# Masks of two attention units as four matmuls on 32-row tiles, and keys' one-hot clusters turned two tiles at a time

## The chip, the cores and the metric

The kernel runs on one core of one Trainium2 chip. The metric is the device time of one execution in microseconds (us), as the median of repeated runs. Engines are named as in the profile: PE is TensorE (matmuls), PEld its weight loads, DVE VectorE, ACT ScalarE, POOL GpSimd, SP SyncE; SPq and POOLq are the queues that issue DMAs.

## The reference

An attention whose mask comes from clusters, and then a mixture of experts. Cut to what matters here:

```python
# q, k, v: (4, 8, 768, 64), centroids: (8, 16, 64)
q_assign = np.argmax(np.einsum('bhsd,hcd->bhsc', q_n, c_n), axis=-1)
k_assign = np.argmax(np.einsum('bhsd,hcd->bhsc', k_n, c_n), axis=-1)
mask = q_assign[:, :, :, None] == k_assign[:, :, None, :]
scores = np.where(mask, scale * (q @ k.T), -1000000000.0)
attn = softmax(scores); x = attn @ v
# then: each of the 3072 tokens goes to one of 8 experts (argmax of a cosine),
out = gate * (relu(x @ w1[e]) @ w2[e])      # w1: (8, 512, 1024), w2: (8, 1024, 512)
```

A query sees the keys that fall into its own cluster, of 16.

## The kernel before, in words

**Stages.** Attention first (to about 445 us), then the routing tables (to about 478 us), then 28 blocks of 128 tokens through the experts (to the end). The change touches the attention alone.

**Rounds, units and groups.** Heads are worked two at a time: a round is one batch and one pair of heads, 16 rounds in all (`pairs`). The 768 tokens are six tiles of 128 (NJ = 6, tile j). A unit (`units`) is one round, one half of the queries (hq, 384 columns) and one tile j of 128 keys, for both heads; there are 192. Six units with the same half of the queries are a group (GU), whose output gathers in one bank `o_ps`.

**The mask as a matmul.** For each token, head, and queries or keys, `oh` holds a one-hot row of its cluster, and in column C a constant (−1 for queries, +1 for keys). Turned by TensorE, they become `qH` and `kH`, with each head's clusters on partitions of their own; `qH` is multiplied by 2^60 on the way (L283). The product kH·qH is then 0 where clusters agree and −2^60 where they don't, and the scores are added to it in the same bank. In `oh` each tile and head has 64 columns (D), of which 17 are used, so a tile of 128 tokens turns into 128 partitions, head 0 on 0 to 63 and head 1 on 64 to 127; `turn_hot` (L272) makes six transposes for the queries and six for the keys.

**A unit.** `scores(i)` (L330 to 345) issues two bf16 mask matmuls (one per head, 64 contraction rows each, 384 columns) and two f32 score matmuls (kT, qT) on the same 64-row tiles, into the two banks of one `s_ps` buffer; there are two such buffers (`psS`, bufs=2), so a unit's mask waits for the exponential of the unit two before. `expo(i)` (L347) takes the exponential on ScalarE. `attend(i)` (L352) multiplies by the values on TensorE and adds up the probabilities on VectorE (`acc`, L367 and L377). At a group's end `total` (L381) sums `acc` over partitions on TensorE, ScalarE copies it (L393), and `divide` (L396) takes the reciprocal (L401) and writes `xT` (L402) on VectorE. `rows` (L413) turns it back.

**The preparation of the next round** is cut into ten pieces (`prep_pieces`, list at L309): turns of q and k with copies by ScalarE (L227) and VectorE (L229), `products` with the centroids (L235), `assign` (turn L248, maximum L256, equality L257, and on GpSimd a preference that breaks ties, L258), `choose` (maximum L264, one-hot L265), nothing, `turn_hot` of queries (copy on VectorE L283), `turn_hot` of keys (copy on ScalarE L285), and `mean` (L298, L306), which is added to the output so that an empty row becomes the mean of the values.

**The order is written out by hand** (`manual_schedule`, L515, for TensorE, VectorE and ScalarE). The loop at L524 takes two units per iteration, six iterations per round: scores and exponentials of the two units ahead, a piece of the preparation, every third iteration `rows` of the last group, `attend` of the two units at hand, every third iteration `total` and `divide`, a second piece, and in some rounds a piece of the routing (`route_pieces`, L430 to 505). So of a round's iterations the first two hold the turns and products, the third `assign` and `choose`, the fourth the queries' `turn_hot` at its end, the fifth the keys' `turn_hot` and `mean`. Small outputs of TensorE share two banks (`misc`, bufs=2), used in turn.

Engines take their instructions in order, so whatever stands behind a waiting one waits too.

Of the kernel before, what the change touches and what calls it, by code (L numbers as in the profile page):

```python
# [9 lines left out]
F32 = mybir.dt.float32  # L10
BF16 = mybir.dt.bfloat16
# [24 lines left out]
def kernel(  # L36
# [67 lines left out]
    with ExitStack() as at:  # L104
# [61 lines left out]
        nc.vector.tensor_scalar(tok_t, tok_i, 6, None, ALU.arith_shift_right)  # L166
        nc.vector.tensor_scalar(tok_hi, tok_t, 1, None, ALU.add)

        ohs = [const.tile([P, NJ // 2, 4, 2, D], BF16, name=f"oh{i}") for i in range(2)]
        for oh in ohs:  # L170
            nc.gpsimd.memset(oh, 0.0)
            for t in range(2):
                nc.gpsimd.memset(oh[:, :, 2 * t : 2 * t + 2, :, C : C + 1], (-1.0, 1.0)[t])

        def unit_rows(dst, src, n):

# [32 lines left out]
        def prep_pieces(n):  # L209

            hp = pairs[n][1]
            t = ld[n]
            oh = ohs[n % 2]

            def turn(nm, half):
                if half == 0:
                    t[nm + "T"] = trp.tile([P, S], F32, tag=nm + "T", name=nm + "T")
                bk = misc()
                for j in range(NJ // 2):
                    nc.tensor.transpose(  # L220
                        bk[:, P * j : P * j + P],
                        t[nm][:, NJ // 2 * half + j].rearrange("p h d -> p (h d)"),
                        ident,
                    )
                dst = t[nm + "T"][:, HS * half : HS * half + HS]
                if nm == "q":
                    nc.scalar.activation(dst, bk[:, 0:HS], ACTF.Copy, scale=scale)  # L227
                else:
                    nc.vector.tensor_copy(dst, bk[:, 0:HS])  # L229

            def products():

                bk = misc()
                for i in range(4):
                    nc.tensor.matmul(  # L235
                        bk[2 * C * i : 2 * C * i + 2 * C, 0:HS],
                        lhsT=cnB[:, hp],
                        rhs=t["qk"[i // 2] + "T"][:, HS * (i % 2) : HS * (i % 2) + HS],
                        start=True,
                        stop=True,  # L240
                    )
                t["asT"] = smp.tile([P, HS], F32, tag="asT", name="asT")
                nc.scalar.copy(t["asT"], bk[:, 0:HS])

            def assign():
                bk = misc()
                for u in range(NJ // 2):
                    nc.tensor.transpose(  # L248
                        bk[:, P * u : P * u + P], t["asT"][:, P * u : P * u + P], ident
                    )  # L250
                shp = [P, 4 * NJ, C]
                asn = bk[:, 0 : 4 * NJ * C].rearrange("p (g c) -> p g c", c=C)
                amax = smp.tile(shp[0:2], F32, tag="amax", name="amax")
                sel = smp.tile(shp, BF16, tag="sel", name="sel")
                t["sel"] = sel
                nc.vector.tensor_reduce(amax, asn, axis=AXX, op=ALU.max)  # L256
                nc.vector.tensor_tensor(sel, asn, bc(amax, shp, 2), ALU.is_equal)  # L257
                nc.gpsimd.tensor_tensor(sel, sel, bc(prefc, shp, 1), ALU.mult)  # L258

            def choose():  # L260

                shp = [P, 4 * NJ, C]
                pm = smp.tile(shp[0:2], BF16, tag="pm", name="pm")
                nc.vector.tensor_reduce(pm, t["sel"], axis=AXX, op=ALU.max)  # L264
                nc.vector.tensor_tensor(  # L265
                    oh.rearrange("p u t h c -> p (u t h) c")[:, :, 0:C],
                    t["sel"],
                    bc(pm, shp, 2),
                    ALU.is_equal,
                )  # L270

            def turn_hot(i, nm):  # L272
                hot = t[nm + "H"] = trp.tile([P, S], BF16, tag=nm + "H", name=nm + "H")
                bk = misc().bitcast(BF16)
                for j in range(NJ):
                    half, u = divmod(j, NJ // 2)
                    nc.tensor.transpose(
                        bk[:, P * j : P * j + P],
                        oh[:, u, 2 * i + half].rearrange("p h c -> p (h c)"),
                        identb,  # L280
                    )
                if nm == "q":
                    nc.vector.tensor_scalar(hot, bk[:, 0:S], BIG, None, ALU.mult)  # L283
                else:
                    nc.scalar.copy(hot, bk[:, 0:S])  # L285

            def values():

                v = t["v"]
                vs = smp.tile([P, NJ // 2, 2, D], F32, tag="vs", name="vs")  # L290
                nc.gpsimd.tensor_tensor(vs, v[:, 0 : NJ // 2], v[:, NJ // 2 :], ALU.add)  # L291
                nc.gpsimd.tensor_tensor(vs[:, 0], vs[:, 0], vs[:, 1], ALU.add)
                nc.gpsimd.tensor_tensor(vs[:, 0], vs[:, 0], vs[:, 2], ALU.add)
                t["vs"] = vs

            def mean():
                bk = misc()
                nc.tensor.matmul(  # L298
                    bk[:, 0:1],
                    lhsT=t["vs"][:, 0].rearrange("p h d -> p (h d)"),  # L300
                    rhs=epsc,
                    start=True,
                    stop=True,
                )
                t["ev"] = smp.tile([P, 1], F32, tag="ev", name="ev")
                nc.vector.tensor_copy(t["ev"], bk[:, 0:1])  # L306


            return [  # L309
                lambda: (turn("q", 0), turn("k", 0), values()),  # L310
                lambda: turn("q", 1),
                lambda: turn("k", 1),
                products,
                assign,
                choose,
                None,
                lambda: turn_hot(0, "q"),
                lambda: turn_hot(1, "k"),
                mean,
            ]  # L320

# [7 lines left out]

        def scores(i):  # L330

            n, hq, j = units[i]
            t = ld[n]
            s_ps = un[i]["s_ps"] = psS.tile([P, 2, 512], F32, tag="s_ps", name="s_ps")
            for l, r, first in (("kH", "qH", True), ("kT", "qT", False)):
                for h in range(2):
                    rows = slice(D * h, D * h + D)
                    nc.tensor.matmul(  # L338
                        s_ps[:, h, 0:HS],
                        lhsT=t[l][rows, P * j : P * j + P],  # L340
                        rhs=t[r][rows, HS * hq : HS * hq + HS],
                        start=first,
                        stop=not first,
                    )

        def expo(i):
# [168 lines left out]
        with tc.manual_schedule(engines={EngineType.PE, EngineType.DVE, EngineType.Activation}):  # L515
            for piece in prep_pieces(0):
                if piece:
                    piece()
            for m in range(2):
                scores(m)  # L520
                expo(m)


            for i in range(0, len(units) + 6, 2):  # L524
                g, part = divmod(i, GU)
                if i < len(units) and i % (2 * NJ) == 0:
                    n = i // (2 * NJ)
                    assert not prepare
                    if n + 1 < len(pairs):
                        load(n + 1)  # L530
                        prepare = prep_pieces(n + 1)
                    if n == 1:

                        for w in range(2):
                            nc.sync.dma_start(
                                out=w1s[w], in_=moe_w1[0].rearrange("(c p) f -> p c f", p=P)
                            )
                            nc.sync.dma_start(
                                out=w2s[w], in_=moe_w2[0].rearrange("(c p) d -> p c d", p=P)
                            )  # L540
                for m in range(i + 2, min(i + 4, len(units))):
                    scores(m)
                    expo(m)
                prep()
                if part == 4 and g > 0:
                    rows(g - 1)
                for m in range(i, min(i + 2, len(units))):
                    attend(m)
                if part == 0 and g > 0:
                    total(g - 1)  # L550
                    divide(g - 1)
                prep()
                if routing:
                    routing.pop(0)()
                if part == 4 and g > 0 and g % (2 * NHP) == 0:
                    assert not routing
                    routing = route_pieces(g // (2 * NHP) - 1)
# [252 lines left out]
```

## Time and profile before

| what | value |
|---|---|
| median of five runs | 904.37 us (903.69 to 905.53) |
| the profiled execution's own time | 904.47 us |
| its span, first to last instruction | 902.70 us |
| TensorE matmul busy | 842.4 us (93%) |
| TensorE weight loads busy | 495.5 us (55%) |
| VectorE busy | 357.1 us (40%) |
| ScalarE busy | 301.7 us (33%) |
| GpSimd busy | 127.6 us (14%) |
| score matmuls L338, f32 | 768 records, 486 ns each |
| mask matmuls L338, bf16 | 384 records, 329 ns each |
| turns of one-hot rows L277 | 192 records |

How to read it: busy times are unions of records, and matmul records overlap, since a matmul is shown from its start to a modelled end; the distance from one start to the next tells for how long the array was taken. An f32 matmul is two records, each with a weight load of its own. In a row, "64*128" is the shape of the array's part that is used (rows by columns), "64x384" the moving operand. Times in the timeline count from the first instruction. The TensorE clock is full (1.00) in the attention stage from about 24 us on.

### The profile page before, as it was taken

The numbers are of one execution on the slowest core, as the hardware profiler recorded it, in microseconds if no ns is written. First come the engines' busy times: TensorE is split into PE (matmuls) and PEld (weight loads), VectorE is DVE, ScalarE is ACT, GpSimd is POOL, SyncE is SP. The second block draws the span as 40 slices with busy tenths as digits, with TensorE's granted clock in tenths as the row PEclk, the third lists the DMA queues.
The fourth block names the chain that finished last, engine by engine and source line by source line (L and its number), as shares of the span: only waits on it lengthen the run. The fifth ranks groups of instructions, "written<-read, shape, count | busy, mean of one in ns | idle before, by whom it ended". The sixth has DMA issues, their size and how long they took to land.

```text
span 902.7 us, 12774 instructions
## 1 busy us (share of the span) xinstructions
PE 842.4 (93%) x5207; PEld 495.5 (55%) x5207; DVE 357.1 (40%) x488; ACT 301.7 (33%) x485; POOL 127.6 (14%) x171
## 2 busy tenths in 40 slices
PE   4999999999999999999628999999999999999996
PEld 2444444444444444444216777767676776767672
DVE  3577777877777877687750000000000000000000
ACT  3545556654566555755330111111111111111110
POOL 4011010211111111110021011110101010101010
PEclk8999999999999999999957999999999999999998
DMA  9822211322213122020011390756565656405610
GB/s 241 308 54 53 53 36 36 108 53 53 53 36 106 36 54 53 19 88 1 1 70 36 117 321 24 261 192 256 192 256 189 260 199 258 152 24 199 233 36 21
DMA packets 105645, 106.85 MB, mean 118 GB/s; under 512 B 77157, under 2 KB 77157, under 8 KB 105072
## 3 DMA queue, kind: packets, MB, share of 16 engines
q1 hardware_dynamic: 100928, 92.30, 32.1%
q0 software_dynamic: 4480, 13.65, 4.1%
q8 instruction: 43, 0.70, 0.3%
q14 instruction: 18, 0.15, 0.0%
q10 hardware_dynamic: 176, 0.05, 0.0%
HBM read 152.11 MB, written 13.64 MB: 184 GB/s over the span
## 4 chain that ended last, share of the span: by engine, by line
PE 38%; issue 29%; DMA 19%; DVE 9%; ACT 2%; POOL 1%; SPq 0%; POOLq 0%; DVEq 0%
DMA out_dram<-y,sidx 19%; PE s_ps L338 15%; PE o_ps L358 12%; DVE den L401 4%; PE misc L220 3%; PE misc L385 2%; PE misc L235 2%; PE misc L419 1%; DVE acc L377 1%; DVE xT L402 1%; ACT den L393 1%; PE misc L441 1%; PE misc L248 1%; DVE qH L283 1%; PE misc L298 1%
## 5 line engine op out<-in xcount | busy, mean ns | idle before, releaser
L714 PEld LDWEIGHTS h_ps<-xTm,w1s 128*128 128x128 f32 x1792 | 204.7, 193 | 22.1 <-DVE xTm L704 19.7
L714 PE MATMUL h_ps<-xTm,w1s 128*128 128x128 f32 x1792 | 208.8, 278 | 3.0 <-DMA w1s<-in_moe_w_dram 3.0
L727 PE MATMUL y_ps<-w2s,hT 128*128 128x512 f32 x448 | 201.2, 592 | 0.0
L349 ACT ACTIVATE prob<-s_ps 128x768 f32<-128x768 f32 x192 | 153.2, 811 | 100.4 <-PE s_ps L338 78.1
L704 DVE COPY xTm<-x_ps 128x512 f32<-128x512 f32 x28 | 19.4, 691 | 381.0 <-PE x_ps L702 381.0
L338 PE MATMUL s_ps<-qT,kT 64*128 64x384 f32 x768 | 156.5, 486 | 0.0
L358 PE MATMUL o_ps<-prob,v 128*64 128x384 f32 x768 | 145.1, 499 | 0.0
L377 DVE TENSOR_TENSOR acc<-acc,prob 128x768 f32<-128x768 f32 x128 | 130.2, 1017 | 4.9
L727 PEld LDWEIGHTS y_ps<-w2s,hT 128*128 128x128 f32 x448 | 81.0, 190 | 81.3 <-issue 81.3
L721 ACT ACTIVATE hT<-h_ps 128x512 f32<-128x512 f32 x56 | 33.4, 597 | 243.8 <-PE h_ps L714 243.8
L401 DVE RECIPROCAL den<-den 128x384 f32<-128x384 f32 x32 | 81.7, 2552 | 30.8 <-ACT den L393 30.8
L338 PEld LDWEIGHTS s_ps<-qT,kT 64*128 64x128 f32 x768 | 69.3, 190 | 21.4 <-issue 21.4
L736 POOL DMA_INDIRECT out_dram<-y,sidx x28 | 28.4, 1014 | 356.4 <-ACT y L735 350.4
L358 PEld LDWEIGHTS o_ps<-prob,v 128*64 128x64 f32 x768 | 46.5, 136 | 56.7 <-issue 55.1
L338 PE MATMUL s_ps<-qH,kH 64*128 64x384 bf16 x384 | 64.0, 329 | 1.6 <-ACT prob L349 1.3
L735 ACT ACTIVATE y<-y_ps,xin 128x512 f32<-128x512 f32 x28 | 19.2, 687 | 136.1 <-PE y_ps L727 129.9
L291 POOL TENSOR_TENSOR vs<-v 128x384 f32<-128x384 f32 x16 | 17.2, 1073 | 221.6 <-DMA v<-in_v_dram 221.6
L338 PEld LDWEIGHTS <-kH 64*128 64x128 bf16 x384 | 19.4, 94 | 51.7 <-issue 37.0
L229 DVE COPY kT<-misc 128x384 f32<-128x384 f32 x32 | 17.7, 554 | 54.1 <-PE misc L220 54.1
L258 POOL TENSOR_TENSOR sel<-sel,prefc 128x384 bf16<-128x384 bf16 x16 | 24.2, 1514 | 102.6 <-DVE sel L257 102.6
L393 ACT COPY den<-misc 128x384 f32<-128x384 f32 x32 | 15.3, 479 | 50.3 <-PE misc L385 50.3
L674 POOL DMA_INDIRECT xin<-x_rows,gidx x28 | 28.9, 1032 | 12.3 <-issue 8.2
(146 smaller groups left out, 511.9 us busy)
## 6 DMA issues: line engine op xcount, KB each, us to landing
w1s<-in_moe_w_dram SPq DMA_DIRECT2D x30, 2048.0 KB
w2s<-in_moe_w_dram SPq DMA_DIRECT2D x30, 2048.0 KB
x_rows<-xr SPq DMA_DIRECT2D x4, 1539.0 KB
q<-in_q_dram SPq DMA_DIRECT2D x32, 192.0 KB
k<-in_k_dram SPq DMA_DIRECT2D x32, 192.0 KB
v<-in_v_dram SPq DMA_DIRECT2D x32, 192.0 KB
xin<-x_rows,gidx POOLq DMA_INDIRECT x28, 6.8
out_dram<-y,sidx POOLq DMA_INDIRECT x28, 7.0
```

Of the source, the lines that this page charges most:

```text
L220: nc.tensor.transpose(bk[:, P * j : P * j + P], t[nm][:, NJ // 2 * half + j].rearrange("p h d -> p (h d)"), ident,)
L338: nc.tensor.matmul(s_ps[:, h, 0:HS], lhsT=t[l][rows, P * j : P * j + P], rhs=t[r][rows, HS * hq : HS * hq + HS], start=first, stop=not first,)
L349: nc.scalar.activation(d["prob"], d["s_ps"][:, :, 0:HS], ACTF.Exp)
L358: nc.tensor.matmul(g["o_ps"][D * h : D * h + D, 0:HS], lhsT=ld[n]["v"][:, j, h], rhs=d["prob"][:, h], start=(j == 0), stop=(j == NJ - 1),)
L377: nc.vector.tensor_tensor(g["acc"], g["acc"], d["prob"], ALU.add)
L393: nc.scalar.copy(d["den"], bk[:, 0:HS])
L401: nc.vector.reciprocal(d["den"], d["den"])
L674: nc.gpsimd.indirect_dma_start(out=xin, out_offset=None, in_=x_rows[:], in_offset=bass.IndirectOffsetOnAxis(ap=gidx[:, j : j + 1], axis=0) ...
L714: nc.tensor.matmul(bk[:, m : m + P], lhsT=w1s[j % 2][:, c, f0 + m : f0 + m + P], rhs=d["xT"][:, P * c : P * c + P], start=(c == 0), stop=( ...
L721: nc.scalar.activation(d["hT"][:, f0 : f0 + 512], bk, ACTF.Relu)
L727: nc.tensor.matmul(bk, lhsT=d["hT"][:, P * c : P * c + P], rhs=w2s[j % 2][:, c], start=(c == 0), stop=(c == KF - 1),)
L736: nc.gpsimd.indirect_dma_start(out=out[:], out_offset=bass.IndirectOffsetOnAxis(ap=sidx[:, j : j + 1], axis=0), in_=y, in_offset=None, bou ...
```

## The change

`scores(i)` now issues two units at once. Their four masks come first, each on a 32-row tile of its own, into the four banks of the two `s_ps` buffers; then the four score matmuls as before, on 64-row tiles. For that `oh` is laid out anew with 32 columns for a tile and head. The queries' one-hot rows are written twice (r = 0, 1), so that a turned tile holds head 0, head 1, head 0, head 1 on four groups of 32 partitions: six transposes as before. The keys' rows are written once, with two tiles side by side in a transpose: three transposes instead of six, and `kH` is half as wide; an even tile j lies on partitions 0 to 63, an odd one on 64 to 127. `choose` writes the one-hot rows by three instructions (twice the queries, once the keys) instead of one. `assign` writes its three turned tiles interleaved, so that the groups lie in the order that the new `oh` wants. The calls of `scores` move: it's called once for two units, ahead of both exponentials, and no longer between them.

```diff
-        ohs = [const.tile([P, NJ // 2, 4, 2, D], BF16, name=f"oh{i}") for i in range(2)]
+        ohs = [const.tile([P, 3 * NJ, 2, 2 * C], BF16, name=f"oh{i}") for i in range(2)]
...
             def assign():
                 bk = misc()
+                tiles = bk[:, 0:HS].rearrange("p (t u w) -> p t u w", t=4, w=2 * C)
                 for u in range(NJ // 2):
-                    nc.tensor.transpose(
-                        bk[:, P * u : P * u + P], t["asT"][:, P * u : P * u + P], ident
-                    )
+                    nc.tensor.transpose(tiles[:, :, u], t["asT"][:, P * u : P * u + P], ident)
...
+                G = 2 * NJ
+                hots = oh.rearrange("p (t j) h c -> p t (j h) c", j=NJ)[:, :, :, 0:C]
+                qs = oh[:, 0:G].rearrange("p (j r) h c -> p j r h c", r=2)[:, :, :, :, 0:C]
+                for r in range(2):
+                    nc.vector.tensor_tensor(
+                        qs[:, :, r],
+                        t["sel"][:, 0:G].rearrange("p (j h) c -> p j h c", h=2),
+                        bc(pm[:, 0:G].rearrange("p (j h) -> p j h", h=2), [P, NJ, 2, C], 3),
+                        ALU.is_equal,
+                    )
                 nc.vector.tensor_tensor(
-                    oh.rearrange("p u t h c -> p (u t h) c")[:, :, 0:C],
-                    t["sel"],
-                    bc(pm, shp, 2),
-                    ALU.is_equal,
+                    hots[:, 2], t["sel"][:, G:], bc(pm[:, G:], [P, G, C], 2), ALU.is_equal
                 )
...
+            def turn_hot_k():
+                hot = t["kH"] = trp.tile([P, HS], BF16, tag="kH", name="kH")
+                bk = misc().bitcast(BF16)
+                for j in range(NJ // 2):
+                    nc.tensor.transpose(
+                        bk[:, P * j : P * j + P],
+                        oh[:, 2 * NJ + 2 * j : 2 * NJ + 2 * j + 2].rearrange("p j h c -> p (j h c)"),
+                        identb,
+                    )
+                nc.scalar.copy(hot, bk[:, 0:HS])
...
         def scores(i):
-            n, hq, j = units[i]
-            t = ld[n]
-            s_ps = un[i]["s_ps"] = psS.tile([P, 2, 512], F32, tag="s_ps", name="s_ps")
-            for l, r, first in (("kH", "qH", True), ("kT", "qT", False)):
+            for m in (i, i + 1):
+                un[m]["s_ps"] = psS.tile([P, 2, 512], F32, tag="s_ps", name="s_ps")
+            for m in (i, i + 1):
+                n, hq, j = units[m]
                 for h in range(2):
-                    rows = slice(D * h, D * h + D)
+                    r = D * (j % 2) + 2 * C * h
                     nc.tensor.matmul(
-                        s_ps[:, h, 0:HS],
-                        lhsT=t[l][rows, P * j : P * j + P],
-                        rhs=t[r][rows, HS * hq : HS * hq + HS],
-                        start=first,
-                        stop=not first,
+                        un[m]["s_ps"][:, h, 0:HS],
+                        lhsT=ld[n]["kH"][r : r + 2 * C, P * (j // 2) : P * (j // 2) + P],
+                        rhs=ld[n]["qH"][r : r + 2 * C, HS * hq : HS * hq + HS],
+                        start=True,
+                        stop=False,
+                    )
+            for m in (i, i + 1):
+                n, hq, j = units[m]
+                for h in range(2):
+                    nc.tensor.matmul(
+                        un[m]["s_ps"][:, h, 0:HS],
+                        lhsT=ld[n]["kT"][D * h : D * h + D, P * j : P * j + P],
+                        rhs=ld[n]["qT"][D * h : D * h + D, HS * hq : HS * hq + HS],
+                        start=False,
+                        stop=True,
                     )
...
+                if i + 2 < len(units):
+                    scores(i + 2)
                 for m in range(i + 2, min(i + 4, len(units))):
-                    scores(m)
                     expo(m)
```

The clears of `oh` on GpSimd follow its new shape, and the queries' turn (`turn_hot_q`) keeps its six transposes and its copy with the factor 2^60.

More of the change, by code (lines that the diff above doesn't have):

```diff
@@ L167 @@
         nc.vector.tensor_scalar(tok_hi, tok_t, 1, None, ALU.add)
-        ohs = [const.tile([P, NJ // 2, 4, 2, D], BF16, name=f"oh{i}") for i in range(2)]
+        ohs = [const.tile([P, 3 * NJ, 2, 2 * C], BF16, name=f"oh{i}") for i in range(2)]
         for oh in ohs:
             nc.gpsimd.memset(oh, 0.0)
-            for t in range(2):
-                nc.gpsimd.memset(oh[:, :, 2 * t : 2 * t + 2, :, C : C + 1], (-1.0, 1.0)[t])
+            nc.gpsimd.memset(oh[:, 0 : 2 * NJ, :, C : C + 1], -1.0)
+            nc.gpsimd.memset(oh[:, 2 * NJ :, :, C : C + 1], 1.0)
         def unit_rows(dst, src, n):
@@ L265, in choose, with turn_hot_q @@
                 nc.vector.tensor_tensor(
-                    oh.rearrange("p u t h c -> p (u t h) c")[:, :, 0:C],
-                    t["sel"],
-                    bc(pm, shp, 2),
-                    ALU.is_equal,
-                )
-            def turn_hot(i, nm):
-                hot = t[nm + "H"] = trp.tile([P, S], BF16, tag=nm + "H", name=nm + "H")
+                    hots[:, 2], t["sel"][:, G:], bc(pm[:, G:], [P, G, C], 2), ALU.is_equal
+                )
+            def turn_hot_q():
+                hot = t["qH"] = trp.tile([P, S], BF16, tag="qH", name="qH")
@@ L274, in turn_hot @@
                 bk = misc().bitcast(BF16)
                 for j in range(NJ):
-                    half, u = divmod(j, NJ // 2)
                     nc.tensor.transpose(
                         bk[:, P * j : P * j + P],
-                        oh[:, u, 2 * i + half].rearrange("p h c -> p (h c)"),
+                        oh[:, 2 * j : 2 * j + 2].rearrange("p r h c -> p (r h c)"),
                         identb,
                     )
[L282 to L285, printed above, removed]
+                nc.vector.tensor_scalar(hot, bk[:, 0:S], BIG, None, ALU.mult)
@@ L316, in prep_pieces @@
                 None,
-                lambda: turn_hot(0, "q"),
-                lambda: turn_hot(1, "k"),
+                turn_hot_q,
+                turn_hot_k,
                 mean,
@@ L518 @@
                     piece()
+            scores(0)
             for m in range(2):
-                scores(m)
                 expo(m)
@@ L540 @@
                             )
+                if i + 2 < len(units):
+                    scores(i + 2)
                 for m in range(i + 2, min(i + 4, len(units))):
-                    scores(m)
                     expo(m)
```

## The prediction

> **What bounds the kernel now.** I read the busy table first, then the stretches, then single instructions. In the attention stage (25 to 445 us) TensorE is busy 98% of each 100 us and no other engine passes 76%:
>
> ```profile
> core 0: us, PE busy (x) PEld busy (x) DVE busy (x) ACT busy (x) POOL busy (x), PEclk, DMA share, GB/s
> 100.00:200.00 100.00, 98.00 (x662) 44.90 (x660) 74.24 (x95) 56.51 (x93) 15.53 (x22) 1.00 0.25 64
> 200.00:300.00 100.00, 97.60 (x662) 45.06 (x661) 75.59 (x95) 56.82 (x93) 13.64 (x21) 1.00 0.25 64
> ```
>
> So a change to TensorE's instructions counts here, except where TensorE already waits. The expert stage after 480 us is not touched. The timeline of TensorE shows the pair of units that the change rewrites (start, length, instructions; the mask is the bf16 row):
>
> ```profile
> 204.08 0.35 PE L298 MATMUL misc<-epsc,vs 128*128 128x1 f32 x2 [0.41 <-DVE qH L283]
> 204.36 0.34 PE L338 MATMUL s_ps<-qH,kH 64*128 64x384 bf16 x2
> 204.53 0.81 PE L338 MATMUL s_ps<-qT,kT 64*128 64x384 f32 x4
> 205.18 0.33 PE L338 MATMUL s_ps<-qH,kH 64*128 64x384 bf16 x2
> 205.34 0.81 PE L338 MATMUL s_ps<-qT,kT 64*128 64x384 f32 x4
> 206.08 0.55 PE L419 MATMUL misc<-ident,xT 128*128 128x128 f32 x3
> 206.56 0.54 PE L358 MATMUL o_ps<-prob,v 128*64 128x384 f32 x2
> ```
>
> Only starts can be subtracted, since the matmuls overlap. Two masks occupy the array 0.16 us (205.18 to 205.34): the two heads run side by side on two 64-row tiles. An f32 matmul is two records of 0.32 us, again both heads side by side, so a unit's scores take 0.64. With 0.17 for the first mask, a pair of units takes 0.173 + 0.645 + 0.163 + 0.642 = 1.623 us. There are 96 such pairs.
>
> **What a change of tile shape costs.** By the single records, the last score record above starts at 205.668 and streams 0.32, but the transposes (128*128) start at 206.082: 0.094 of gap. The same gap stands wherever the shape in the rows changes: last transpose 206.357 + 0.109 to the value matmul (128*64) at 206.559 is 0.093; last value record 207.584 + 0.322 to the mask (64*128) at 208.003 is 0.097; 128*64 to 128*32 (L358 to L235) 0.094. Where the shape stays (L358 to L385, both 128*64) there is none: 211.543 to 211.866 is just the 0.32. And after a change the first weight load isn't hidden:
>
> ```profile
> 204.04 0.30 PEld L298 LDWEIGHTS misc<-epsc,vs 128*128 128x128 f32 x2 [1.05 <-issue]
> 204.36 0.10 PEld L338 LDWEIGHTS <-kH 64*128 64x128 bf16 x2
> ```
>
> These two f32 loads of 128 columns serve matmuls of one column, so the 0.313 from 204.045 to 204.358 is two loads and one change: (0.313 − 0.095)/2 = 0.109 a load. For 64 f32 columns the trace agrees: value records after a change are 0.374 apart instead of 0.322, so 0.052. A bf16 load of 128 columns shows only 0.01 (mask to scores 0.172 instead of 0.162).
>
> **The change, part by part.**
> (1) Masks (96 pairs). The second unit's masks leave their place: −0.163. Four masks on 32-row tiles start some 3 ns apart, as the two do now: +0.006. New is a change of shape between masks (32*128) and scores (64*128), which today share 64*128. No row shows 32 rows against 64, so I bound it: nothing, by the L358 to L385 row, or 0.094 and a visible f32 load of 0.105 (twice the 0.052, and near the 0.109), together 0.199. I take the upper end: rows with a change of row height alone (128*128 to 64*128, L220 to L338: 205 ns less 109) pay 0.096 like the rest. The pair becomes −0.163 + 0.006 + 0.199 = **+0.042 us**. That four masks run at once isn't shown for rows; four 32-column tiles do (L235 starts three of them 6 ns apart), so I take 0.16 for all four; the other end is two after two, +0.16 more.
>
> The Trainium skill speaks against this change: "TensorEngine Tiling (Array Packing)", Key Properties, says that a change of tiling mode, not of tile, drains the array, which fits the 0.09 of the rows and would give the 32-to-64 step the same. "TensorE: Matmul & The Clock Gate", Part 3, measures four row tiles at 3.07 times rather than 4; as an estimate by that page a group of four masks would take 0.64/3.07 = 0.21 us rather than 0.16, and the pair +0.09. No run here shows either.
>
> (2) Where a pair's price is hidden. TensorE waits for VectorE at two places in each round of six score pairs (one head pair of a batch). The first: the mean (L298) takes the bank that qH's copy leaves, which stands behind the reciprocal:
>
> ```profile
> 200.18 2.55 DVE L401 RECIPROCAL den<-den 128x384 f32<-128x384 f32 x1 [0.57 <-ACT den L393]
> 202.85 0.62 DVE L402 SCALAR_TENSOR_TENSOR xT<-o_ps,ev,den 128x384 f32<-128x384 f32 x1
> 203.38 0.55 DVE L283 TENSOR_SCALAR qH<-misc 128x768 bf16<-128x768 bf16 x1
> ```
>
> In 12 of 15 rounds the mean starts 0.48 to 0.58 late. It is fixed by the totals (L385) 5.27 us before, so the one score pair and the keys' turn between them gain and cost nothing. The second: the fourth product (L235) starts 0.22 late, for kT's copy, behind the round's other reciprocal; that hides one score pair in each of the 15 rounds. In three rounds (routing) VectorE also holds the turn of qH (L277, after the choice), which hides one pair each; and the last pair runs beside the final reciprocal (437.51). So 15 + 12 + 3 + 1 = 31 hidden, and the two pairs before 26 us are counted apart: 63 × 0.042 = **+2.65 us**.
>
> (3) The keys' turn: three transposes less of 0.055 each (six take 0.33, from 201.72) = 0.16; visible only in the three rounds without a wait at the mean: **−0.5**. The kH copy (ScalarE, 0.79) halves, off the path.
>
> (4) The choice: one 384-element is_equal becomes three of 192.
>
> ```profile
> 198.18 0.56 DVE L265 TENSOR_TENSOR oh<-sel,pm 128x384 bf16<-128x384 bf16 x1
> 198.66 0.95 DVE L367 SCALAR_TENSOR_TENSOR acc<-prob 128x768 f32<-128x768 f32 x1
> ```
>
> Now 0.48 from start to start, of which some 0.40 goes with the elements; three of 0.28 make 0.83, with waits among them 1.07: +0.35 to +0.59 (at most +1.24, if size saves nothing). Behind it stand the accumulation and the reciprocal, which starts 0.57 after VectorE is free: hidden in the usual rounds. In the three routing rounds VectorE has no gap and the turn follows the choice by 57 ns: 3 × 0.47 = **+1.4**. If the cover went in nine usual rounds too, 1.24 would cost 9 × 0.67 = 6 us.
>
> (5) The wait that is moved. The first mask of the second unit now stands ahead of all scores, and waits for the exponential two units back. Today that has ended 0.94 us or more before the pair starts in nearly all iterations (0.51 in one):
>
> ```profile
> 205.45 1.61 ACT L349 ACTIVATE prob<-s_ps 128x768 f32<-128x768 f32 x2 [2.12 <-PE s_ps L338]
> ```
>
> It ends at 207.06; the next masks start at 208.00. The first unit now finishes 0.2 later, so both exponentials end some 0.2 later: still on time. In the three routing rounds it ends 0.65 after the pair's start; queued behind are all scores, but TensorE waited 0.65 after that anyway (totals 0.48, turn 0.17), for VectorE, which (4) has charged. In the prologue the second pair started at 23.82, while the second exponential ended at 24.86: all its scores now come after that, so the 0.64 of one unit no longer fills the wait, plus 0.2 for the change of shape: **+0.9** (bounds 0.6 to 1.2).
>
> (6) The strided writes of the three turned tiles, and smaller clears of oh on GpSimd (1.37 each, at 2.7 to 5.3 us, needed at 17.4): nothing; at most a few hundredths in a place that waits.
>
> **Sum:** +2.65 − 0.5 + 1.4 + 0.9 = +4.45. The profiled execution took 904.47 (span 902.70 and 1.77 around it): 908.9. It stands 0.1 above the median 904.37 of the five runs: **908.8**.
>
> **Rivals.**
> (A) Free change of height: masks and scores both split by rows, and the array takes 32 rows against 64 like one shape. A pair then saves 0.163 − 0.006 = 0.157: 63 × 0.157 = 9.9 less, with the other terms (+1.8) −8.1: **896**. For it: no row shows this step. Against: every change of either number in the rows pays. It decides from a price below 0.157 − 1.8/63 = 0.128 us for a change.
> (B) The change costs only its gap, the load slips in behind the masks: 0.157 − 0.094 = 0.063 saved, 63 × 0.063 = 4.0, with +1.8 −2.2: **902**. Against: no load in the rows starts before the gap's end.
> (C) The four masks don't run together, but two after two: 0.042 + 0.160 = 0.202, 63 × 0.202 = 12.7, +1.8: **919**. For it: two tiles at most are seen in the rows' direction. Against: four column tiles do, and the masks go to four banks.
>
> **Chances.** Forecast 0.68, B 0.11, A 0.12, C 0.09. The range reaches down over A and B (896 less 1) and up over the forecast with most of a dear choice (908.8 + 4); left out are C (0.09) and some 0.07 at the ends of the others: 895 to 913. The forecast's own range is 906 to 913. By 0.2% (1.8 us, about what a measurement of this kernel can tell from no change): faster 0.12 and 0.07 of B, 0.19; same 0.04 of B and 0.06 of the forecast's low end, 0.10; slower 0.71.
>
> **What would show it.** Right: four mask starts within 0.01; first scores 0.26 to 0.27 after the first mask instead of 0.17; the first unit's second records 0.43 after its first, not 0.32; a pair 1.66; waits at the mean a little shorter; three is_equal of about 0.36. Wrong: scores 0.17 after the mask (A); 0.27, but then 0.32 (B); mask starts in two groups 0.16 apart (C); or a mask waiting for prob in usual rounds, against (5).

## The result, and the profile after

The changed kernel takes 906.41 us in the median (905.46 to 909.09, 29 runs) against 904.47 (902.88 to 906.03, 49 runs) for the kernel before on the same chips: a ratio of 1.0027 (95% interval 1.0022 to 1.0032; the two medians alone give 1.0021): slower by little, but clear of the noise. Of its 29 runs 16 have a granted TensorE clock of 0.972 to 0.976 and take 905.46 to 906.85, and 13 have 0.968 to 0.970 and take 906.72 to 909.09. Its profiled execution is one of the shorter ones: 906.31 us with a span of 904.27, so 1.57 more span than before. The forecast was slower, 908.8 with a range of 895 to 913: the sign and the range held, the size was 2.4 too much.

From the page of the changed kernel: the span, the busy table, and two groups of part 5 (busy time, mean ns of one, idle time before them).

```profile
span 904.3 us, 12711 instructions
PE 843.7 (93%) x5159; PEld 489.8 (54%) x5159; DVE 362.9 (40%) x520; ACT 288.6 (32%) x485; POOL 127.0 (14%) x171
...
L364 PE MATMUL s_ps<-qT,kT 64*128 64x384 f32 x768 | 151.2, 512 | 0.0
```

A mean f32 score record is 512 ns long instead of 486, although the same work is done: the first two score records of each pair now include something that isn't streaming (587 ns each in the pair below; the other six have 482 or 483). TensorE's timeline of the pair that the prediction worked out shows what (start, length, instructions):

```profile
206.67 0.35 PE L314 MATMUL misc<-epsc,vs 128*128 128x1 f32 x2 [0.53 <-DVE qH L290]
206.96 0.34 PE L354 MATMUL s_ps<-qH,kH 32*128 32x384 bf16 x4
207.23 1.56 PE L364 MATMUL s_ps<-qT,kT 64*128 64x384 f32 x8
208.72 0.55 PE L445 MATMUL misc<-ident,xT 128*128 128x128 f32 x3
```

By the single records the four masks start at 206.958, .962, .965 and .968. The scores start 0.27 after the first mask (0.17 before), and the first unit's second records 0.427 after its first (0.322). So the four masks do run at once, and the array then pays a gap and one f32 weight load that nothing covers. The pair takes 1.665 us, before 1.623: +0.042, as predicted to the third digit.

VectorE's timeline of the same round, around the choice:

```profile
200.74 0.63 DVE L269 TENSOR_TENSOR oh<-sel,pm 128x192 bf16<-128x192 bf16 x2
201.28 0.35 DVE L275 TENSOR_TENSOR oh<-sel,pm 128x192 bf16<-128x192 bf16 x1
201.55 0.95 DVE L393 SCALAR_TENSOR_TENSOR acc<-prob 128x768 f32<-128x768 f32 x1
202.78 2.55 DVE L427 RECIPROCAL den<-den 128x384 f32<-128x384 f32 x1 [0.28 <-ACT den L419]
```

The three is_equal take 0.81 from start to start instead of 0.48, and the gap ahead of the reciprocal shrinks from 0.57 to 0.28: hidden here, as predicted. The list of TensorE's waits (us in total, times, longest) tells the rest. First after, then before:

```profile
PE misc L314 <- DVE qH L290: 7.9, 13, 0.9
...
PE h_ps L741 <- DMA w1s<-in_moe_w_dram: 0.4, 1, 0.4
```

```profile
PE misc L298 <- DVE qH L283: 5.2, 12, 0.5
...
PE h_ps L714 <- DMA w1s<-in_moe_w_dram: 3.0, 5, 0.8
```

The first line grew, where the prediction had the waits at the mean "a little shorter" (taken up further down). The second line of each is a surprise: the change touches nothing of the experts, and yet their wait for weights fell from 3.0 to 0.4.

**Where the time went.** Lining up the same instruction in both traces:

| place | before, us | after, us | shift | predicted |
|---|---|---|---|---|
| masks of the first pair | 20.64 | 21.05 | +0.40 | in the +0.9 |
| masks of the third pair | 28.55 | 29.82 | +1.27 | +0.9 |
| masks of the 95th pair | 433.08 | 437.56 | +4.48 | |
| routing tables (sidx) | 472.91 | 477.44 | +4.53 | +4.45 |
| turns of the expert stage's block 2 | 503.60 | 508.00 | +4.40 | |
| block 9 | 605.69 | 609.74 | +4.04 | |
| block 12 | 650.44 | 653.66 | +3.22 | |
| block 15 | 694.99 | 697.59 | +2.60 | |
| block 21 | 783.71 | 785.44 | +1.72 | |
| end | 902.70 | 904.27 | +1.57 | +4.45 |

In this pair of executions the attention costs what was forecast. From the routing tables on 3.0 us come back, 2.8 of it in five steps of the expert stage (−0.36, −0.82, −0.62, −0.87, −0.14), all at places where the kernel before waits for weights. The experiments had two questions: is the pair's price the change of tile height, and why do the experts give time back?

### The profile page after: what moved, and what is told of

The parts are those of the page before. It is cut to its first block, busy times and chain, and to the rows that moved or that the text cites. A ratio compares the mean times of both kernels' runs of the same rounds, so it can differ in the third digit from the quotient of the medians.

```text
span 904.3 us, 12711 instructions
## 1 busy us (share of the span) xinstructions
PE 843.7 (93%) x5159; PEld 489.8 (54%) x5159; DVE 362.9 (40%) x520; ACT 288.6 (32%) x485; POOL 127.0 (14%) x171
## 4 chain that ended last, share of the span: by engine, by line
PE 38%; issue 28%; DMA 19%; DVE 10%; ACT 2%; POOL 1%; SPq 0%; POOLq 0%; DVEq 0%
DMA out_dram<-y,sidx 19%; PE s_ps L364 13%; PE o_ps L384 12%; DVE den L427 4%; PE misc L221 3%; PE s_ps L354 2%; PE misc L411 2%; PE misc L236 2%; DVE acc L403 1%; PE misc L445 1%; DVE xT L428 1%; PE misc L467 1%; ACT den L419 1%; DVE qH L290 1%; PE misc L250 1%
## 5 line engine op out<-in xcount | busy, mean ns | idle before, releaser
L375 ACT ACTIVATE prob<-s_ps 128x768 f32<-128x768 f32 x192 | 145.3, 809 | 123.1 <-PE s_ps L364 99.9
L364 PE MATMUL s_ps<-qT,kT 64*128 64x384 f32 x768 | 151.2, 512 | 0.0
L364 PEld LDWEIGHTS s_ps<-qT,kT 64*128 64x128 f32 x768 | 66.6, 187 | 41.9 <-issue 17.4
L763 POOL DMA_INDIRECT out_dram<-y,sidx x28 | 28.4, 1014 | 353.4 <-ACT y L762 347.5
L354 PE MATMUL s_ps<-qH,kH 32*128 32x384 bf16 x384 | 34.4, 334 | 2.8 <-ACT prob L375 2.8
L354 PEld LDWEIGHTS <-kH 32*128 32x128 bf16 x384 | 10.3, 91 | 41.0 <-issue 39.6
L393 DVE SCALAR_TENSOR_TENSOR acc<-prob 128x768 f32<-128x768 f32 x32 | 30.4, 950 | 0.0
```

The lines of the kernel that those rows point to most:

```text
L354: nc.tensor.matmul(un[m]["s_ps"][:, h, 0:HS], lhsT=ld[n]["kH"][r : r + 2 * C, P * (j // 2) : P * (j // 2) + P], rhs=ld[n]["qH"][r : r + 2 ...
L364: nc.tensor.matmul(un[m]["s_ps"][:, h, 0:HS], lhsT=ld[n]["kT"][D * h : D * h + D, P * j : P * j + P], rhs=ld[n]["qT"][D * h : D * h + D, H ...
L375: nc.scalar.activation(d["prob"], d["s_ps"][:, :, 0:HS], ACTF.Exp)
L393: nc.vector.scalar_tensor_tensor(out=g["acc"], in0=un[i - 1]["prob"], scalar=NJ * EPS, in1=d["prob"], op0=ALU.add, op1=ALU.add,)
L763: nc.gpsimd.indirect_dma_start(out=out[:], out_offset=bass.IndirectOffsetOnAxis(ap=sidx[:, j : j + 1], axis=0), in_=y, in_offset=None, bou ...
```

## The experiments

### The price of the tile height

**mask32_each**: the kernel before, unit by unit, with masks on 32 rows; rows 32 to 63 hold zeros.

```diff
-                    rows = slice(D * h, D * h + D)
+                    rows = slice(D * h, D * h + (2 * C if first else D))
```

> The kernel before, with each mask matmul cut to the 32 of its 64 rows that hold clusters (the other 32 are zero), unit by unit, in the same places of the array; nothing else differs. Theory (a change between 32 and 64 rows costs a change of shape): each unit pays 0.20 ahead of its scores, and the second unit 0.11 to go back, +0.50 per pair; 63 pairs fully and 27 beyond what their waits hide: +31 to +38. Rival (height is free): within 1 of the kernel before.

Measured: 942.01 us (one run), every uncovered pair +0.50, the routing tables 37.5 late. TensorE's timeline:

```profile
225.38 0.33 PE L338 MATMUL s_ps<-qH,kH 32*128 32x384 bf16 x2
225.64 0.92 PE L338 MATMUL s_ps<-qT,kT 64*128 64x384 f32 x4
226.49 0.34 PE L338 MATMUL s_ps<-qH,kH 32*128 32x384 bf16 x2
```

Masks to scores 0.26 to 0.27, the scores 0.92 instead of 0.81, and back to the masks 0.10 more than streaming takes (all by the single records' starts). A change from 32 to 64 rows costs 0.20 (gap and load), the way back 0.10; a pair has two of the first and one more of the second than it had, 0.50. It is the height alone, since nothing else differs.

**after_mask64**: the changed kernel with masks of 64 rows again. Each mask then adds up both heads' clusters, so a query sees other keys and the tokens are routed otherwise; only the attention's time is compared.

```diff
-                    r = D * (j % 2) + 2 * C * h
+                    r = D * h
...
-                        lhsT=ld[n]["kH"][r : r + 2 * C, P * (j // 2) : P * (j // 2) + P],
+                        lhsT=ld[n]["kH"][r : r + D, P * (j // 2) : P * (j // 2) + P],
```

(and the same for qH.)

> The changed kernel with each mask as a 64-row matmul (it adds up both heads' clusters, so which keys a query sees is changed, and the routing of tokens too); the order, oh, choice and turns of the change stay. Theory: without the change of shape a pair is 1.62 again, 0.042 less: the routing tables (sidx) come 2.4 to 3.0 earlier than in the changed kernel, some 1.8 after the kernel before. Rival (the masks' height has no part in it): within 0.5 of the changed kernel.

Measured: 902.15 us (one run). The routing tables come at 473.65, 3.79 earlier than after; the pairs cost exactly what they did before (+0.00), and 1.02 of the 3.79 lies in the prologue (third pair at 28.80 instead of 29.82), which is why it is more than the 2.4 to 3.0 expected. The other 2.77 are 64 pairs of 0.04. Against the kernel before, the rounds differ only by the choice and the keys' turn. So the pairs' +2.8 is the height.

**order_only**: the kernel before with the masks of two units first, on 64 rows: the order of the change without its tiles.

```diff
             for l, r, first in (("kH", "qH", True), ("kT", "qT", False)):
-                for h in range(2):
+                for m in (i, i + 1):
+                    for h in range(2):
```

(and `scores` called once for two units.)

> The kernel before, with the four masks of two units ahead of their scores, on the 64-row tiles as before; layout, choice and turns as before. Theory (the price of the change is the new shape change): a pair stays at 1.62 us, and only the prologue's wait for the second exponential is new, +0.6 to +0.9 at the routing tables (sidx). Rival (the moved wait is what costs): most of the 4.5, +3 to +4.5.

Measured: 905.08 (10 runs), ratio 1.0008 (0.9997 to 1.0018). The third pair is 0.6 late (two executions of the kernel before differ by 0.14 there), and from there every pair +0.00 to the end of the attention: the moved wait for the exponential costs 0.6 once, in the prologue, and nothing in a round.

### Why the experts give time back

**nw_before, nw_after**: both kernels without the loads of expert weights in the expert stage: all blocks use the first expert's weights, which are loaded ahead of it. So nothing there waits for weights.

```diff
-            weights(j)
...
-            if j + 2 < j1:
-                weights(j + 2)
```

> The kernel before, with the experts' weights never reloaded (all blocks use the first expert's weights, so the expert outputs are not the reference's; the instructions of TensorE, VectorE and ScalarE are the same). Theory: in the profile of before, TensorE waits 3.0 us for weights in the expert stage; without reloads those go, so some 901.5 (2.5 to 3.5 less than before). Rival: the waits of that profile are an accident of one execution; then this is up to 1 us from before.

> The changed kernel, with the experts' weights never reloaded, as in the run nw_before. Theory: the attention stage is 4.4 to 4.6 longer with the change, and the measured 1.9 is smaller because the changed kernel happens to wait less for weights; so this is 4.2 to 4.8 above nw_before, and only 0 to 0.7 below the changed kernel. Rival: the attention costs less in usual executions than in the profiled one; then 1.5 to 2.5 above nw_before.

Measured: 902.24 (11 runs, ratio to the kernel before 0.998, 0.9971 to 0.9989) and 908.19 (5 runs, 1.0046, 1.0032 to 1.006). The medians lie 5.95 apart instead of the 4.2 to 4.8 expected, and the second is above the changed kernel, not below it; the prologue, whose length varies (see before_again and after_again), is in them, so the profiled executions are compared. Without the loads the change costs 5.3 in the profiled spans (899.57 to 904.86) instead of 1.57: 4.42 at the routing tables, and 0.86 once, at the expert stage's start, where TensorE's clock is still half (37.5 us of it, from 445.1 in one and 451.3 in the other, so to 9.6 and 11.5 us after the routing tables). After that every block is +0.00. So what the experts give back goes with the loads of weights: it is the wait for them.

**before_again, after_again**: both kernels once more, for a second trace.

> The kernel before, profiled once more. Theory that the waits for weights go with the kernel: again 2 to 4 us of waits of the first layer's matmuls for weights after 480 us, and the same attention stage within 0.2. Rival that they go with the execution: anything from 0 to 4.

> The changed kernel, profiled once more. Theory that the waits for weights go with the kernel: again 0 to 1 us of waits for weights, and the routing tables ready (sidx) at 477.4 within 0.2, which is 4.5 after the kernel before. Rival that they go with the execution: waits anywhere from 0 to 4.

Measured: 903.70 and 908.35 (one run each). By the distances of the records' starts, the waits for weights are 3.2 us in six places and 0.5 in one (first traces: 3.4 in five and 0.4 in one): they belong to the kernels, not to an execution. But the routing tables come at 479.40 in the second execution of the changed kernel, not at 477.4 within 0.2 as expected: 6.2 after those of before_again (473.19). The 2 us lie in the prologue, ahead of the third pair, which comes at 31.77 instead of 29.82; from there to the 95th pair both executions agree within 0.01. In the prologue TensorE runs at half its clock for a stretch. In after_again the clock's records give that until 30.2 us; in the first execution they begin only at 24.6, with the full clock, and ahead of that its score records start 0.64 apart instead of 0.32, so there too it ran at half.

**after_pad**: the first candidate was the place of the expert tiles in memory, which the smaller `oh` moves by 1536 bytes a partition.

```diff
+        const.tile([P, 768], BF16, name="pad")
```

> The changed kernel with 1536 unused bytes per partition behind oh, so that every tile of the expert stage lies at the address that it has in the kernel before (the new oh is smaller, which had moved them). Theory: the waits for weights after 480 us follow from these addresses; with the pad they return, 2.5 to 3.5 us in five or six places, and the kernel is 4 to 5 above the one before. Rival: they follow from the moment at which the stage begins, or from something else that the change moves; then 0 to 1 us of waits, as in the changed kernel, and 1.5 to 3.5 above the kernel before.

Measured: 907.78 (5 runs), 1.0038 (1.0024 to 1.0052), wait for weights still 0.5. Not the addresses.

**What differs at a load.** The views of the DMA queues, over the time in which the expert stage loads two weight tiles and TensorE then needs the second (packets, MB, share). Before, 622 to 637 us; then after, 625.6 to 641:

```profile
DMA packets 1732, 4.75 MB, mean 317 GB/s; under 512 B 64, under 2 KB 64, under 8 KB 1730
...
q8 instruction: 1, 0.02, 0.4%
q14 instruction: 1, 0.01, 0.1%
```

```profile
DMA packets 1757, 4.78 MB, mean 311 GB/s; under 512 B 64, under 2 KB 64, under 8 KB 1756
...
q14 instruction: 1, 0.01, 0.1%
```

Both have one of 8 KB on queue 14. Before also has a packet on queue 8 in this stretch, after has none: 16 KB of instructions, at 630.5, which take about 1 us of a DMA engine while weights keep the engines busy (0.9 to 1.6 us by the packets' own records). 6.7 us later TensorE waits 0.85 for these weights. In after the nearest such packets are at 619.0, before these loads begin, and at 645.4, when the tiles that TensorE waits for have landed. The pattern holds over eleven traces of kernels that load weights and route alike. Of 41 loads of two tiles (the first of each kernel aside) with an instruction packet in the first 15 us, 38 are followed by a wait of 0.29 to 1.12 us; of 25 loads without one, none is. (The first load of each kernel has a packet 5 to 11 us in and no wait.)

The packets come by the count of instructions: three blocks are 504 TensorE instructions, and two packets come with them, so about 256 each. The change has 96 TensorE instructions less in the attention (48 transposes with their 48 weight loads). That moves all later packets. It is the count and not the moment: mask32_each, whose expert stage begins 37.5 us later than in the kernel before with as many instructions, has its packets 5 to 9 us into the same loads, and five waits again. Two kernels test it.

**after_6turns**: the changed kernel with 96 TensorE instructions put back, three useless transposes in each keys' turn.

```diff
+                for j in range(NJ // 2):
+                    nc.tensor.transpose(
+                        bk[:, HS + P * j : HS + P * j + P],
+                        oh[:, 2 * NJ + 2 * j : 2 * NJ + 2 * j + 2].rearrange("p j h c -> p (j h c)"),
+                        identb,
+                    )
                 nc.scalar.copy(hot, bk[:, 0:HS])
```

> The changed kernel with the three key transposes that it saves put back as repeats into unused columns, so that TensorE has as many instructions as in the kernel before (96 more than the change: 48 transposes and their weight loads). Two things are asked. First, the saved turns are hidden in 12 of 15 rounds: the routing tables (sidx) come 0.3 to 1.0 later than in the changed kernel, not 2.6. Second, theory on the waits for weights after 480 us: a fetch of 16 KB of instructions falls into the load of a block's weights and holds one of its DMA engines up for about 1 us; where the fetches fall goes with the number of TensorE's instructions, so the waits return, 2.5 to 3.5 us in five or six places, and the kernel is 4 to 6 above the one before. Rival (the waits go with anything else of the change): 0 to 1 us of waits, 1.5 to 4 above.

Measured: 909.74 (5 runs), 1.0056 (1.0043 to 1.007). The routing tables come 1.29 later than in after, more than the 0.3 to 1.0 expected, since 0.82 of it is the prologue (third pair at 30.64, half clock until 28.4); the turns themselves cost 3 × 0.17. From the routing tables to the end another 2.2 is lost. TensorE's waits:

```profile
PE h_ps L747 <- DMA w1s<-in_moe_w_dram: 2.8, 6, 0.7
```

**before_plus5**: the kernel before with 160 TensorE instructions more (five useless transposes a round). 160 more is 96 fewer, if 256 make a packet.

```diff
+                if nm == "k":
+                    for j in range(5):
+                        nc.tensor.transpose(
+                            bk[:, S + P * (j % 2) : S + P * (j % 2) + P],
+                            oh[:, 0, 2 * i].rearrange("p h c -> p (h c)"),
+                            identb,
+                        )
```

> The kernel before with five useless transposes after the keys' turn in each round (repeats into unused columns): 160 instructions of TensorE more, which shifts the later ones against the 256 of a 16 KB fetch as 96 fewer do. The 0.28 us of each round stands in the gap ahead of the mean (0.48) in most rounds: the routing tables (sidx) come 0.5 to 1.7 later. Theory (fetches among the loads of weights): the waits after 480 us fall from some 3.2 to below 1, and the whole is 1 to 2.5 faster than before although it does more. Rival: the waits stay, and the whole is 0.5 to 1.7 slower.

Measured: 903.46 (11 runs), 0.9986 (0.9977 to 0.9995): a kernel that only does more is a little faster. The routing tables are 1.04 late, and the experts give 2.3 back:

```profile
PE h_ps L721 <- DMA w1s<-in_moe_w_dram: 0.6, 1, 0.6
```

Both came as the packets said, in opposite directions. That the place of the packets, by the count of instructions, decides on the waits is shown. That a packet delays the weights behind it on its DMA engine is inferred from the times, since which of the 16 engines was late isn't in the trace.

### The wait at the mean

**late_mean_before**: the kernel before with the mean one iteration later. TensorE waits 5.2 us in 12 rounds where the mean stands.

```diff
                 lambda: turn_hot(1, "k"),
+                None,
+                None,
                 mean,
```

> The kernel before with the mean (L298) one iteration later in each round, after the copy of qH has long ended. Theory: TensorE's gap ahead of the mean, 0.48 to 0.58 in 12 of 15 rounds, goes and nothing takes its place: the routing tables (sidx) 5 to 6.5 earlier, and the whole 4 to 7 below the kernel before. Rival (VectorE, which is busy from the reciprocal on, makes TensorE wait elsewhere in the round): less than 2 earlier.

Measured: 904.54 (11 runs), 0.9999 (0.999 to 1.0008). The gain of 4 to 7 us that I expected isn't there:

```profile
PE s_ps L340 <- DVE qH L283: 5.2, 12, 0.5
```

The same 5.2 us in 12 waits now stand at the masks. The prediction had read the wait as the mean's, for a bank. But the next round's masks, which come right behind the mean, need `qH` itself. The mean was only the first to meet a copy that is late for everyone.

**q_before_recip**: the copy is late because it stands in VectorE's order behind the reciprocal. Here the second piece of the preparation comes between `total` and `divide`; and, to place the instruction packets, 80 useless transposes (160 TensorE instructions) go where TensorE waits 10.6 us for the routing anyway. The base is the kernel before.

```diff
                     total(g - 1)
+                prep()
+                if part == 0 and g > 0:
                     divide(g - 1)
-                prep()
...
+            fill = misc().bitcast(BF16)
+            for s in range(80):
+                nc.tensor.transpose(fill[:, P * (s % 4) : P * (s % 4) + P], identb, identb)
             inv = misc()[:, 0 : 2 * NBLK]
```

> The kernel before with two edits that the other runs point to. First, the queries' clusters are turned (and copied by VectorE, line 283) ahead of the division of the group before, not behind it: in the kernel before the turned clusters are ready at 40.92 us of the first round, but the copy stands in VectorE's order behind the 2.55 us reciprocal and the 0.62 us multiplication and starts only at 44.25. Second, 80 useless transposes of the identity are put ahead of the routing tables' matmuls, where TensorE waits 10.6 us for VectorE anyway; these 160 TensorE instructions shift the instruction fetches of the expert stage as before_plus5 did. If the wait of the mean and of the next masks is the place of the copy in VectorE's order (late_mean_before had the same 5.2 us in 12 waits, at the masks instead of the mean), then those 12 waits of about 0.43 us go: the routing tables come 5 us earlier (468 instead of 472.9), and if the fetches decide the waits for weights these fall from 3.0 to 0.7 us: together 895 to 897 us. If something else is as late as the copy, the attention stage stays within 1 us of before and the time is 901 to 903. If the reciprocal, now 0.5 us later, holds up the rows of the group before, the wait stands there and the gain is smaller again.

Measured: 896.11 us (895.72 to 896.53, 4 runs) against 904.45: 0.9907 (0.989 to 0.9923). It beats both kernels. VectorE's timeline of the round that the prediction showed:

```profile
197.49 0.56 DVE L283 TENSOR_SCALAR qH<-misc 128x768 bf16<-128x768 bf16 x1 [0.49 <-PE misc L277]
197.96 2.54 DVE L401 RECIPROCAL den<-den 128x384 f32<-128x384 f32 x1
200.54 0.62 DVE L402 SCALAR_TENSOR_TENSOR xT<-o_ps,ev,den 128x384 f32<-128x384 f32 x1
```

The copy comes first, in a gap of VectorE, the reciprocal starts directly behind it, and of TensorE's waits this is what stays:

```profile
PE h_ps L718 <- DMA w1s<-in_moe_w_dram: 0.7, 1, 0.7
...
PE misc L298 <- DVE qH L283: 0.2, 1, 0.2
```

The twelve waits are gone (−0.45 in nine rounds, −0.55 in three; the routing tables come at 466.68 instead of 472.91), and the experts give another 2.2.

## Why the prediction was right, and where it failed

**Right: the pair.** +0.042 was forecast from gaps between other shapes and from a load seen elsewhere, and +0.042 was measured; 64 pairs show it (2.8 us in all, forecast 63 and 2.65), three of them beside the shorter turn of the keys, and 23 are hidden where the prediction named the cover, most of them behind the mean's wait and ahead of the products. Rival A fell (32 rows against 64 isn't free: mask32_each), B fell (the second record 0.427 after the first, so the load isn't covered), and so did C (the masks start 3 to 4 ns apart). The Trainium skill's rule that a change of tiling mode drains the array ("TensorEngine Tiling (Array Packing)", Key Properties) agrees with the rows here; it names no price, and a little over half of the 0.20 is not the gap of 0.094 but the f32 load behind it (0.105). The estimate of 0.21 us for four masks, from the 3.07 times for four row tiles in "TensorE: Matmul & The Clock Gate", Part 3, doesn't fit: from the first mask to the first score it is 0.270 with four masks, and 0.264 with two in mask32_each, so four take 0.006 more than two.

**Right in sum, partly by luck.** The prologue: +1.27 measured against +0.9, outside its bounds of 0.6 to 1.2. The part between the first and the third pair is +0.87; the +0.40 ahead of the first mask was left out, and the choice's three instructions stand there (the wait for `oh` grew from 3.7 to 4.0). But the first mask's time differs by 1.1 us between two executions of the kernel before (20.64 and 19.54), so this isn't settled. The prediction also gave the stretch at half clock no part in the prologue's cost. That stretch ends between 23.8 and 25.4 us in six traces of kernels whose score instructions are those of the kernel before, but at 24.6, 30.2 and 30.4 in after, after_again and after_pad, whose third pairs come at 29.82, 31.77 and 31.93. By the second traces of both kernels the prologue costs +3.4 and the attention +6.2, with the same +3.2 from the third to the 95th pair. Why the stretch is longer in some executions stays open. The choice in the routing rounds: 3 × 0.34 against 3 × 0.47. The keys' turn: 3 × −0.17 against 3 × −0.16. The sum to the routing tables, +4.53 against +4.45, is closer than its terms: prologue and pairs came out dearer, the choice cheaper.

**Wrong: one sentence.** The step that failed is "The expert stage after 480 us is not touched." Its instructions are not, but 96 TensorE instructions fewer ahead of it moved the instruction packets out of the loads that TensorE waits for: −2.8 us in five steps, in place of 0, more than half of what the attention lost. The profile of before had the sign of it: a wait of 3.0 us for weights in five places, although the stage loads two weight tiles in the same way in seven, and a queue named "instruction". A wait behind some of several like loads has a cause beside the loads.

**Misread without harm:** the mean's wait "takes the bank that qH's copy leaves". It is the copy that is late, for the masks too. The prediction's sum used only that the wait was there. Nor did the waits get "a little shorter": they grew from 0.41 to 0.53 us in nine rounds, since VectorE sets the mean's time and the keys' turn ahead of it lost 0.17 while the pair gained 0.04; and from 0.50 to 0.90 in three, where the dearer choice also delays the copy.

## What to carry to other kernels

Price a matmul's tile shape against its neighbours' on the engine: here a smaller tile saved 0.16 us of streaming and paid 0.20 for the change of height, so the split lost. When a wait goes, look at who needs the same result next: moving the mean moved the wait, and only moving the copy ahead of the reciprocal removed it. And when an untouched stage changes its time, compare the instruction packets' places before looking for a cause in its data.

## What the runs showed of the hardware that was not expected

- TensorE's instructions arrive by DMA in packets of 16 KB (about 256 instructions, 0.9 to 1.6 us each), while the kernel's own loads run. After one in the first 15 us of a load of two tiles, TensorE waited 0.29 to 1.12 us for weights in 38 of 41 cases; 160 useless instructions more made the kernel 0.14% faster (0.9986, 0.9977 to 0.9995).
- A change from 32-row to 64-row tiles costs some 0.09 to 0.10 us (0.264 from mask to score in mask32_each, where 0.16 is streaming) and exposes the first weight load behind it (0.105 for 128 f32 columns); back to 32 rows with bf16 costs 0.10.
- The prologue's stretch at half the TensorE clock varies between executions of one kernel: in the changed kernel it lasts until 24.6 us in one and until 30.2 in another (profiled executions 906.31 and 908.35).
